# Attention and MLP kernel: weight loads in written order, six staging buffers, VectorE and ScalarE by hand in batch 0, and k, q, p turned on VectorE

## The chip, the cores and the metric

The kernel runs on one core of one Trainium2 chip. The metric is device time in microseconds (us) of one execution. A core has four engines that matter here: TensorE (PE, matrix products; PEld is its weight load), VectorE (DVE), ScalarE (ACT) and GpSimd (POOL), and SyncE (SP), whose queue issues all the DMA transfers of this kernel. Each engine works through its own list of instructions in order and waits at semaphores for the others.

## The reference

Eight batches, eight heads, 576 positions, 64 wide. Each head has 32 rows p, which attend to k and v; q then attends to the 32 packed rows. The heads side by side are the input of an MLP with the function h * tanh(softplus(h)).

```python
def sm_attn(qq, kk, vv):
    s = scale * np.matmul(qq, kk.transpose(0, 1, 3, 2))
    s = s - np.max(s, axis=-1, keepdims=True)
    a = np.exp(s)
    a = a / (np.sum(a, axis=-1, keepdims=True) + 1e-09)
    return np.matmul(a, vv)
p_packed = sm_attn(p, k, v)
out = sm_attn(q, p_packed, p_packed)
...
h = x @ w_in                      # 4608 x 512 @ 512 x 2048
sp = np.where(h > 20.0, h, np.log1p(np.exp(np.minimum(h, 20.0))))
g = h * np.tanh(sp)
return (g @ w_out).astype(np.float32)
```

q, k, v, p are float32; w_in and w_out are float64 and are made float32 on the chip.

## The kernel before, in words

**Weights.** A piece of a weight matrix is 128 x 512 float64, loaded as 128 x 1024 int32 into a staging buffer `w_st` (L343 for w_in, L370 for w_out; three buffers, `STB`). ScalarE takes its two words apart (`words`, L350 and L351), VectorE joins them into a float32 (`join`, four instructions in a chain on the same tile: L355, L358, L359, L362). There are 32 pieces: 16 of w_in (named wi) and 16 of w_out (named wo).

**Attention.** k and q come as tiles of 96 partitions (`load_heads`, L103, 288 KB a transfer). PE transposes them in blocks of four (`transposed`, L129), and ScalarE or VectorE copies each block out of PSUM (L119 to L123). p is transposed by PE too (L177) and copied by VectorE (L180, L183). Then PE makes the scores (L138); VectorE takes the maximum and subtracts it (L192 to L196); ScalarE takes the exponentials (L231) and VectorE their sums (L232); PE transposes the weights (`turn_weights`, L241, twelve per batch) and makes the packed rows (`values`, L250); these are scaled (L258), transposed (L266) and copied (L267) into ppT. The second half multiplies ppT with qT (L138), turns the result with VectorE's own transposes (`match`, L281), normalizes (`peak` and `weigh`, L289 to L302), turns it back (L307), and splits it in a high and a low part, aT_hi on ScalarE (L308) and aT_lo on VectorE (L309).

**MLP.** The packed rows stand before the weights: `packed_w` (L380) multiplies ppT with a quarter of w_in and splits the result into wp_hi (ScalarE, L391) and wp_lo (VectorE, L392). There are four quarters a batch. A group (b, f) is one batch and 128 of the 2048 hidden columns: `up` makes 2 x 6 products of 288 columns (L430), ScalarE applies the function (L433, L435), and from batch 1 on `halves` splits the result into g_hi (L444) and g_lo (L445) on VectorE. `down` multiplies with w_out: in batch 0 in float32 (L469), later as three split products (L449, L450, L451). The split of w_out (wo_hi on ScalarE, L92, and wo_lo on VectorE, L93) stands in batch 1's loop. Every sixteenth group `evac` copies four accumulators into `o` (three buffers) and out. Each batch leaves 64 of its 576 positions over; two batches' rests are multiplied together (L449 to L451 with the names r_hi, r_lo, ps_rest).

**Order.** After batch 0's attention the loop runs over t = 0 .. 129: up of group t, down of group t - 2, and between them up to three steps of the next batch's attention, a generator. PE's order is as written throughout. The other engines are ordered by hand through batch 0's attention, and after it by the tile scheduler, which by its own estimate places each engine's instructions. In batch 0's loop each step converts two pieces.

## Time and profile before

| | |
|---|---|
| median of 3 runs | 825.61 us (821.64 to 1091.88) |
| profiled execution | 823.42 us |
| its span | 821.5 us |
| PE busy | 768.5 us (94%) |
| PE weight load busy | 592.8 us (72%) |
| VectorE busy | 407.3 us (50%) |
| ScalarE busy | 335.0 us (41%) |
| DMA by SP's queue | 55.59 MB, 24.0% of 16 engines' span |

The profile is one execution. The span runs from the first instruction to the last; the execution's time is 1.92 us longer. In a row of the timeline stand the start, the duration, the engine, the line, the operation with its result and operands, the shape, how many follow one another, and in brackets the idle time before it and what ended that. In a row of a group stand the number of instructions, their busy time and mean, and the idle time before them by what ended it. Two PE matmuls overlap, so the distance between their starts is shorter than their durations.

### The profile page before, as it was taken

To read this page: it belongs to the slowest core of one execution; us is meant where nothing else is said; L and a number is where in the kernel's file an instruction comes from. 1 tells how busy PE (TensorE), PEld (TensorE's weight loads), DVE (VectorE), ACT (ScalarE), POOL (GpSimd) and SP (SyncE) were. 2 spreads that over 40 slices of the span, in tenths; PEclk is the share of its full clock that TensorE was granted. 3 is DMA by queue.
4 is the path that set the end of the run, shared out by engine and by line. 5 is a ranking of instruction groups with operands and counts; after the bars stand their busy time and mean duration, and the time that the engine had idled before them with its cause. 6 is when DMAs were issued, how large, how long until landed. Compare 5 with 4: busy or idle time off the path is not lost.

```text
span 821.5 us, 13455 instructions
## 1 busy us (share of the span) xinstructions
PE 768.5 (94%) x5520; PEld 592.8 (72%) x5520; DVE 407.3 (50%) x778; ACT 335.0 (41%) x772; POOL 0.7 (0%) x6
## 2 busy tenths in 40 slices
PE   6527779999999999999999999999999999999997
PEld 4305456557878887877878887877878887888886
DVE  4388787634373344634373444634373444633332
ACT  4156576435342352435342352435342352432221
POOL 0000000000000000000000000000000000000000
PEclk7558999999999999999999999999999999999999
DMA  9826773022300332022300332022300300010002
GB/s 241 214 77 212 235 210 113 1 63 83 86 3 1 102 85 59 1 64 81 88 1 1 102 85 59 1 68 78 88 1 1 100 23 2 1 52 1 1 1 64
DMA packets 34748, 56.43 MB, mean 69 GB/s; under 512 B 7552, under 2 KB 25984, under 8 KB 34688
## 3 DMA queue, kind: packets, MB, share of 16 engines
q1 hardware_dynamic: 34688, 55.59, 24.0%
q8 instruction: 43, 0.70, 0.4%
q14 instruction: 17, 0.14, 0.1%
HBM read 46.14 MB, written 9.44 MB: 68 GB/s over the span
## 4 chain that ended last, share of the span: by engine, by line
PE 86%; DMA 5%; DVE 4%; ACT 3%; issue 1%; SPq 0%; DVEq 0%; ACTq 0%
PE ps_h L430 24%; PE acc L449 14%; PE acc L450 13%; PE acc L451 13%; PE acc L469 5%; DMA w_st<-in_moe_w_in_dram 4%; PE ps_kq L129 4%; PE ps_w L380 4%; PE ps_s L138 3%; PE ps_rest L449 2%; PE ps_rest L450 2%; PE ps_rest L451 2%; PE ps_pp L250 2%; PE ps_a L241 1%; DMA w_st<-in_moe_w_out_dram 1%
## 5 line engine op out<-in xcount | busy, mean ns | idle before, releaser
L433 ACT ACTIVATE g<-ps_h 128x288 f32<-128x288 f32 (+1 forms) x256 | 98.6, 386 | 275.5 <-PE ps_h L430 240.8
L449 PE MATMUL acc<-wo_hi,g_hi 128*128 128x512 f32 x448 | 186.6, 417 | 0.0
L450 PE MATMUL acc<-wo_lo,g_hi 128*128 128x512 f32 x448 | 176.2, 393 | 0.0
L451 PE MATMUL acc<-wo_hi,g_lo 128*128 128x512 f32 x448 | 175.8, 392 | 0.0
L430 PE MATMUL ps_h<-aT_hi,wp_hi 128*128 128x288 f32 x512 | 166.9, 326 | 9.4 <-ACT aT_hi L308 6.3
L444 DVE CAST g_hi<-g 128x512 fp32r<-128x512 f32 x112 | 47.7, 426 | 227.4 <-ACT g L433 227.4
L430 PE MATMUL ps_h<-aT_lo,wp_hi 128*128 128x288 f32 x512 | 152.5, 298 | 0.9 <-DVE aT_lo L309 0.9
L430 PE MATMUL ps_h<-aT_hi,wp_lo 128*128 128x288 f32 x512 | 152.2, 297 | 0.6 <-DVE wp_lo L392 0.6
L430 PEld LDWEIGHTS ps_h<-aT_hi,wp_hi 128*128 128x128 f32 x512 | 97.4, 190 | 30.7 <-issue 10.8
L449 PEld LDWEIGHTS acc<-wo_hi,g_hi 128*128 128x128 f32 x448 | 84.1, 188 | 36.6 <-issue 17.3
L430 PEld LDWEIGHTS ps_h<-aT_lo,wp_hi 128*128 128x128 f32 x512 | 97.6, 191 | 13.6 <-issue 5.0
L451 PEld LDWEIGHTS acc<-wo_hi,g_lo 128*128 128x128 f32 x448 | 84.1, 188 | 19.3
L430 PEld LDWEIGHTS ps_h<-aT_hi,wp_lo 128*128 128x128 f32 x512 | 97.4, 190 | 0.9 <-DVE wp_lo L392 0.9
L450 PEld LDWEIGHTS acc<-wo_lo,g_hi 128*128 128x128 f32 x448 | 84.4, 188 | 7.0
L445 DVE TENSOR_TENSOR g_lo<-g,g_hi 128x512 fp32r<-128x512 f32 x112 | 77.2, 689 | 5.9 <-PE ps_kq L129 0.5
L469 PE MATMUL acc<-wo,g 128*128 128x512 f32 x128 | 64.9, 616 | 0.0
L380 PE MATMUL ps_w<-wi,ppT 64*32 64x512 f32 x512 | 37.7, 615 | 14.9 <-DVE wi L362 14.7
L392 DVE TENSOR_TENSOR wp_lo<-ps_w,wp_hi 128x512 fp32r<-128x512 f32 x64 | 41.2, 681 | 19.1 <-ACT wp_hi L391 19.1
L391 ACT CAST wp_hi<-ps_w 128x512 fp32r<-128x512 f32 x64 | 34.3, 588 | 32.3 <-PE ps_w L380 32.3
L129 PEld LDWEIGHTS ps_kq<-ident,k_t 96*128 96x128 f32 x192 | 20.8, 144 | 18.2 <-issue 6.7
L469 PEld LDWEIGHTS acc<-wo,g 128*128 128x128 f32 x128 | 22.0, 196 | 15.3 <-issue 15.2
L129 PE MATMUL ps_kq<-ident,q_t 96*128 96x96 f32 x192 | 25.6, 264 | 7.6 <-issue 5.2
(93 smaller groups left out, 769.8 us busy)
## 6 DMA issues: line engine op xcount, KB each, us to landing
k_t<-in_k_dram SPq DMA_DIRECT2D x32, 288.0 KB, 3.6
v_t<-in_v_dram SPq DMA_DIRECT2D x32, 288.0 KB, 4.0
q_t<-in_q_dram SPq DMA_DIRECT2D x32, 288.0 KB, 4.3
w_st<-in_moe_w_in_dram SPq DMA_DIRECT2D x16, 512.0 KB, 4.8
w_st<-in_moe_w_out_dram SPq DMA_DIRECT2D x16, 512.0 KB, 4.2
out_dram<-o SPq DMA_DIRECT2D x24, 192.0 KB, 2.2
out_dram<-o SPq DMA_DIRECT2D x16, 128.0 KB, 3.3
out_dram<-o SPq DMA_DIRECT2D x24, 64.0 KB, 2.5
```

The lines of the kernel that those rows point to most:

```text
L129: nc.tensor.transpose(out=ps[:, h, :], in_=of_slot(src, g, h)[:, i, :], identity=ident[:R, :R])
L380: nc.tensor.matmul(out=ps[g][h * NP:(h + 1) * NP, :], lhsT=ppTb[row:row + D, g, h * NP:(h + 1) * NP], rhs=wi[c][g][row:row + D, h // 2, :] ...
L391: nc.scalar.copy(out=hi, in_=ps[g])
L392: nc.vector.tensor_tensor(out=lo, in0=ps[g], in1=hi.bitcast(F32), op=ALU.subtract)
L430: nc.tensor.matmul(out=ps, lhsT=w[:, fs], rhs=a[:, g, cs], start=(n == 0), stop=(n == 5))
L433: nc.scalar.activation(out=self.act[:, hf * HALF:hf * HALF + m], in_=ps[:, :m], func=AF.Mish)
L444: nc.vector.tensor_copy(out=hi, in_=self.act)
L445: nc.vector.tensor_tensor(out=lo, in0=self.act, in1=hi.bitcast(F32), op=ALU.subtract)
L449: nc.tensor.matmul(out=acc, lhsT=hi[:, cs], rhs=wh, start=start, stop=False)
L450: nc.tensor.matmul(out=acc, lhsT=hi[:, cs], rhs=wl, start=False, stop=False)
L451: nc.tensor.matmul(out=acc, lhsT=lo[:, cs], rhs=wh, start=False, stop=stop)
L469: nc.tensor.matmul(out=accs[c], lhsT=grp.act[:, cs], rhs=wo[f], start=f == 0, stop=f == NF - 1)
```

## The change

**Opening.** SP runs by hand, in the order of the program, through the whole of batch 0; VectorE and ScalarE are placed by the scheduler in batch 0's attention, which is written in another order (the first half's second product ahead of the second half's values), and by hand in the loop of batch 0, up to t = 16. There are six staging buffers in place of three. The weights are taken in the order w_in's first quarter, then a piece of w_in and one of w_out by turns; a step joins two, and the words of the piece after are taken behind each join. Batch 0's q, k, v, p lie in a pool `early` of their own, closed at t = 1 (`LOAD0`), when the first three of the later batches' tiles are asked for; the others follow as tiles come free (`load_next`).

**Batches 1 to 7.** A class `Later` loads k and q with 32 columns at a time on 32 partitions (four transfers of 32 x 4 x 544 a tile, in two lanes that overlap, so that they are loaded twice), v on 2 x 64 partitions, p in four transfers. VectorE turns k and q in one STREAM_TRANSPOSE a tile (`lanes`, L374 of the changed kernel, 128 x 1152) and p in one (L368). The weights of the first softmax are turned in ten 128-wide transposes instead of twelve, the packed rows made in 40 matmuls instead of 48 per half. VectorE's work on a PE result is written after the next PE work (`pending`, `flush`).

**Else.** w_out is split from t = 14 on (`SPLIT0`), the first eight into a pool `late`; two output buffers instead of three; rows go out in groups of 64.

```diff
-KVB = 8
-STB = 3
-OB = 3
+KQB = 3
+STB = 6
+OB = 2
+ATT0 = 4
+LOAD0 = 1
+HALFWAY = 8
+SPLIT0 = 14
...
+        def load_side(self, src, g, tag):
+            t = kv[0].tile([P, 4, NX, D], F32, name=tag, tag="kqv", bufs=KQB)
+            for w in range(2):
+                for e in range(2):
+                    lane = (2 * w + e) * NP
+                    rows = src[self.b, 4 * g:4 * g + 4, w * HALF:(w + 1) * HALF].rearrange("h (p x) d -> p h (x d)", x=NX)
+                    nc.sync.dma_start(
+                        out=t[lane:lane + NP].rearrange("p h x d -> p h (x d)")[:, :, :NX * D - NP],
+                        in_=rows[:, :, e * NP:e * NP + NX * D - NP],
+                    )
+            return t
...
+        def lanes(self, src):
+            t = att.tile([P, 4, HALF], F32, name="xT", tag="T", bufs=2)
+            nc.vector.transpose(
+                out=t.rearrange("a h (x n) -> a (h x) n", n=NP),
+                in_=src.rearrange("a h x (e d) -> a (h x) e d", e=2)[:, :, 0, :],
+            )
+            return t
...
-    weights = [Weight(0, m) for m in range(4)] + [WeightOut(0)] + [Weight(1, m) for m in range(4)]
-    weights += [WeightOut(i) for i in range(1, 4)] + [Weight(2, m) for m in range(4)]
-    weights += [WeightOut(i) for i in range(4, 8)] + [Weight(3, m) for m in range(4)]
-    weights += [WeightOut(i) for i in range(8, NF)]
...
+    pieces = [Weight(0, m) for m in range(4)]
+    for f in range(NF):
+        if f < 12:
+            pieces.append(Weight(1 + f // 4, f % 4))
+        pieces.append(WeightOut(f))
...
+    def join_next(n):
+        for _ in range(n):
+            k = pieces_done["join"]
+            upto("words", k + 1)
+            upto("join", k + 1)
+            upto("fetch", k + 1 + STB)
+            upto("words", k + 2)
...
+        by_hand.enter_context(tc.manual_schedule(engines={mybir.EngineType.DVE, mybir.EngineType.Activation}))
+        upto("fetch", 4 + STB)
+        upto("words", 5)
...
-                if f == (0 if b else 2) and b + 1 < B:
+                if f == (1 if b else ATT0) and b + 1 < B:
                     gen = batches[b + 1].attention()
-                if f == 10 and b + 2 < B:
-                    batches[b + 2].load()
+                if t == LOAD0:
+                    opening.close()
+                    kv.append(ctx.enter_context(tc.tile_pool(name="kv", bufs=2, side="left", reuse_waits="tile")))
+                    for _ in range(KQB):
+                        load_next()
...
-            if b == 0:
-                convert(2)
-            elif t == NF:
+            joins = 2 if t < 14 else 0
+            if t == NF:
+                by_hand.close()
+            if t == SPLIT0:
                 stage.close()
-                late.append(ctx.enter_context(tc.tile_pool(name="late", bufs=1)))
-            if b == 1:
-                split_wo(f)
+                late.append(ctx.enter_context(tc.tile_pool(name="late", bufs=1, side="right", reuse_waits="tile")))
+            if 0 <= t - SPLIT0 < NF:
+                split_wo(t - SPLIT0)
```

**What moves on the engines.** On SP, in the opening, before: from the third weight piece (L343 loads w_in, L370 w_out, L103 k, q and v, L165 p).

```order
L343 DMA w_st<-in_moe_w_in_dram 128x1024
L165 DMA p_t<-in_p_dram 128x2x64 x2
L103 DMA q_t<-in_q_dram 96x2x384 x2
L343 DMA w_st<-in_moe_w_in_dram 128x1024
L370 DMA w_st<-in_moe_w_out_dram 128x1024
L103 DMA k_t<-in_k_dram 96x2x384 x4
L103 DMA q_t<-in_q_dram 96x2x384 x2
L343 DMA w_st<-in_moe_w_in_dram 128x1024
L103 DMA q_t<-in_q_dram 96x2x384 x2
L343 DMA w_st<-in_moe_w_in_dram 128x1024 x3
```

The same place now (L521 loads w_in, L548 w_out, L117 batch 0's k, q and v; L355 and L324 the later batches' p, and k and q):

```order
L117 DMA q_t<-in_q_dram 96x2x384 x2
L521 DMA w_st<-in_moe_w_in_dram 128x1024 x3
L548 DMA w_st<-in_moe_w_out_dram 128x1024
L521 DMA w_st<-in_moe_w_in_dram 128x1024
L548 DMA w_st<-in_moe_w_out_dram 128x1024
L521 DMA w_st<-in_moe_w_in_dram 128x1024
L548 DMA w_st<-in_moe_w_out_dram 128x1024
L521 DMA w_st<-in_moe_w_in_dram 128x1024
L548 DMA w_st<-in_moe_w_out_dram 128x1024
L355 DMA p_n<-in_p_dram 32x8x32 x4
L324 DMA k_n<-in_k_dram 32x4x544 x8
L324 DMA q_n<-in_q_dram 32x4x544 x4
```

Batch 1's first k and q, eight transfers, stood ahead of the sixth piece and among those that follow; now its first loads stand behind the twelfth piece, all together.

On VectorE, in the joins of batch 0's loop, before (ISA is the last step of a join, the add, L362; the number in a tile's name tells tiles apart):

```order
L355 TENSOR_SCALAR wo_538<-wo_538 128x512
L362 ISA wo_256<-wo_256,wround 128x1024
L358 TENSOR_SCALAR wo_538<-wo_538 128x512
L359 SCALAR_TENSOR_TENSOR wo_538<-w_st,wo_538 128x512
L355 TENSOR_SCALAR wo_548<-wo_548 128x512
L362 ISA wo_538<-wo_538,wround 128x1024
L358 TENSOR_SCALAR wo_548<-wo_548 128x512
L355 TENSOR_SCALAR wo_576<-wo_576 128x512
```

and now (L533, L536, L537, L540 are the four steps):

```order
L533 TENSOR_SCALAR wo_153<-wo_153 128x512
L536 TENSOR_SCALAR wo_153<-wo_153 128x512
L537 SCALAR_TENSOR_TENSOR wo_153<-w_st,wo_153 128x512
L540 ISA wo_153<-wo_153,wround 128x1024
L533 TENSOR_SCALAR wi_0_93<-wi_0_93 128x512
L536 TENSOR_SCALAR wi_0_93<-wi_0_93 128x512
L537 SCALAR_TENSOR_TENSOR wi_0_93<-w_st,wi_0_93 128x512
L540 ISA wi_0_93<-wi_0_93,wround 128x1024
```

Two joins were interleaved; now each runs through its four steps before the next begins.

On VectorE at the end of batch 0, before: the two wp_lo (L392) of batch 1's first quarter, behind that batch's last attention steps (L302, L307, L309) and two single splits of w_out (L93).

```order
L302 TENSOR_TENSOR a_1258<-a_1258,sm_1327 128x1152
L307 STREAM_TRANSPOSE at<-a_1258 128x576
L93 TENSOR_TENSOR wo_lo<-wo_1216,wo_hi 128x512
L309 TENSOR_TENSOR aT_lo<-at,aT_hi 128x576
L307 STREAM_TRANSPOSE at<-a_1258 128x576
L309 TENSOR_TENSOR aT_lo<-at,aT_hi 128x576
L93 TENSOR_TENSOR wo_lo<-wo_1226,wo_hi 128x512
L392 TENSOR_TENSOR wp_lo<-ps_w_1417,wp_hi 128x512
```

and now (L106 is the split of w_out, L583 of a rest, L570 wp_lo), behind the last join:

```order
L540 ISA wo_1151<-wo_1151,wround 128x1024
L106 TENSOR_TENSOR wo_lo_1317<-wo_153,wo_hi_1316 128x512
L106 TENSOR_TENSOR wo_lo<-wo_807,wo_hi 128x512
L106 TENSOR_TENSOR wo_lo_1390<-wo_476,wo_hi_1389 128x512
L106 TENSOR_TENSOR wo_lo_1420<-wo_514,wo_hi_1419 128x512
L106 TENSOR_TENSOR wo_lo_1485<-wo_575,wo_hi_1484 128x512
L106 TENSOR_TENSOR wo_lo_1562<-wo_619,wo_hi_1561 128x512
L106 TENSOR_TENSOR wo_lo_1618<-wo_678,wo_hi_1617 128x512
L583 TENSOR_TENSOR r_lo<-g_rest_481,r_hi 128x4x64
L106 TENSOR_TENSOR wo_lo_1671<-wo_739,wo_hi_1670 128x512
L106 TENSOR_TENSOR wo_lo<-wo_864,wo_hi 128x512
L570 TENSOR_TENSOR wp_lo<-ps_w_1341,wp_hi 128x512
```

Nine splits of w_out and one of a rest now stand directly ahead of wp_lo, and the last steps of batch 1's attention ahead of the last two joins.

More of the change, by code (lines that the diff above doesn't have):

```diff
@@ L325, in attention, with columns @@
+            self.a2 = att.tile([P, 2, S // NP, NP], F32, name="a2", tag="a", bufs=1)
             for g in range(2):
-                yield from self.values(g, ps_a)
-            for g in range(2):
-                yield from self.turn_values(g, ps_a)
-            for g in range(2):
-                yield from self.match(g, ps_a)
+                self.match(g)
+                yield
+                flush()
+                yield
             self.peak(slice(0, 2))
+            yield
             self.weigh(slice(0, 2))
+        def columns(self, a):
+            return a.rearrange("a (x u n) -> a u x n", u=2, n=NP)
@@ L334, in body, with rows, rest_rows @@
+        def rows(self, c):
+            return [(out_x[self.b, 2 * c + e], e * NQ, (e + 1) * NQ) for e in range(2)]
+        def rest_rows(self):
+            return out_x[self.b, NX - 1]
     class Weight:
@@ L474, in down @@
         o = evac(accs[c], c)
[L475 to L481 removed]
+        for dst, lo, hi in batches[b].rows(c):
+            nc.sync.dma_start(out=dst, in_=o[lo:hi, :])
     rest = {}
@@ L578, in body @@
-        convert(4)
-        batches[1].load()
+        by_hand = ExitStack()
+        by_hand.enter_context(tc.manual_schedule(engines={mybir.EngineType.SP}))
+        first.k_t = [load_heads(k, 0, 0, "k_t")]
+        first.load_p()
+        upto("fetch", 1)
+        first.k_t.append(load_heads(k, 0, 1, "k_t"))
+        first.v_t = [load_heads(v, 0, 0, "v_t")]
+        first.q_t = [load_heads(q, 0, 0, "q_t")]
+        upto("fetch", 2)
+        first.v_t.append(load_heads(v, 0, 1, "v_t"))
+        first.q_t.append(load_heads(q, 0, 1, "q_t"))
@@ new lines, in body @@
+        upto("fetch", STB)
+        first.start(ps_a)
+        score = [first.score_now(g) for g in range(2)]
+        for _ in range(3):
+            next(score[0])
+        upto("words", 1)
+        next(score[0], None)
+        upto("join", 1)
+        next(score[1])
+        next(score[1])
+        together(first.turn_weights(0, ps_acc, ("ACT", "ACT")))
+        next(score[1])
+        next(score[1], None)
+        together(first.values(0, ps_a))
+        together(first.turn(0, ps_acc, ("ACT", "ACT", "ACT")))
@@ new lines, in body @@
+        together(first.turn_values(0, ps_a))
+        together(first.turn_weights(1, ps_acc, ("ACT", "ACT")))
+        together(first.match(0, ps_acc))
+        upto("words", 2)
+        first.peak(slice(0, 1))
+        upto("join", 2)
+        together(first.values(1, ps_a))
+        together(first.turn(1, ps_acc, ("ACT", "ACT", "ACT")))
+        together(first.turn_values(1, ps_a))
+        together(first.match(1, ps_acc))
+        upto("words", 3)
+        first.peak(slice(1, 2))
+        first.weigh(slice(0, 1))
@@ L608, in body @@
                 grp.up(0)
-            next(gen, None)
+            chunk = b == 0 and f % 4 == 3 and f < NF - 1
+            if not chunk:
+                advance(gen)
+            join_next(joins - joins // 2)
             if dn:
```

321 lines of the change are left out of this document (207 added, 114 removed).

## The prediction

> **What bounds the kernel now.** I read the windows first: start:end in us, length, then busy time and (instructions) of PE, of PE's weight loads, VectorE, ScalarE, GpSimd, then the granted clock, the DMA engines' busy share and GB/s.
>
> ```profile
> 0.00:20.00 20.00, 11.92 (x86) 8.69 (x86) 8.59 (x25) 8.33 (x19) 0.70 (x6) 0.80 0.94 240
> 40.00:60.00 20.00, 3.68 (x9) 1.05 (x9) 17.44 (x34) 8.94 (x16) 0.00 (x0) 0.50 0.26 79
> 60.00:80.00 20.00, 14.27 (x71) 9.77 (x71) 17.21 (x37) 13.37 (x28) 0.00 (x0) 0.83 0.67 202
> 80.00:100.00 20.00, 17.33 (x96) 9.60 (x96) 16.74 (x36) 11.90 (x26) 0.00 (x0) 0.91 0.68 221
> 100.00:120.00 20.00, 12.91 (x69) 8.06 (x70) 16.03 (x35) 15.11 (x28) 0.00 (x0) 0.91 0.75 214
> 120.00:140.00 20.00, 20.00 (x180) 12.98 (x181) 17.32 (x35) 16.17 (x38) 0.00 (x0) 1.00 0.52 154
> 640.00:740.00 100.00, 99.98 (x742) 80.75 (x741) 45.15 (x82) 38.42 (x92) 0.00 (x0) 1.00 0.13 37
> ```
>
> There are two programs in one. From 120 us to the end PE is never idle, so a microsecond of PE work removed there is a microsecond of time, as long as nothing new makes PE wait. Before 120 us PE waits, and VectorE is the fullest engine (17.4, 17.2, 16.7, 16.0 of 20). The border between the two I put at the first split matmul of batch 1's second product, which I call T0:
>
> ```profile
> 184.65 0.48 PE L449 MATMUL acc<-wo_hi,g_hi 128*128 128x512 f32 x1
> ```
>
> From T0 to the span's end (821.5) are 636.85 us. The timeline of the opening shows why PE is so late at first:
>
> ```profile
> 38.58 0.66 ACT L350 ACTIVATE wi<-w_st 128x512 f32<-128x512 f32 x1 [9.87 <-DMA w_st<-in_moe_w_in_dram]
> ...
> 39.27 0.43 DVE L355 TENSOR_SCALAR wi<-wi 128x512 f32<-128x512 f32 x1 [9.05 <-ACT wi L350]
> ...
> 57.11 0.78 DVE L307 STREAM_TRANSPOSE at<-a 128x576 f32<-128x576 f32 x1
> ...
> 59.73 0.66 ACT L308 CAST aT_hi<-at 128x576 fp32r<-128x576 f32 x1
> ...
> 60.44 0.61 PE L430 MATMUL ps_h<-aT_hi,wp_hi 128*128 128x288 f32 x1 [6.34 <-ACT aT_hi L308]
> 61.95 0.61 PE L430 MATMUL ps_h<-aT_lo,wp_hi 128*128 128x288 f32 x1 [0.90 <-DVE aT_lo L309]
> 62.35 0.44 PE L430 MATMUL ps_h<-aT_hi,wp_lo 128*128 128x288 f32 x1
> 62.59 0.44 PE L430 MATMUL ps_h<-aT_hi,wp_hi 128*128 128x288 f32 x1
> ...
> 66.80 0.30 PE L430 MATMUL ps_h<-aT_hi,wp_hi 128*128 128x288 f32 x1
> 66.93 0.29 PE L430 MATMUL ps_h<-aT_lo,wp_hi 128*128 128x288 f32 x1
> ```
>
> ScalarE waits 9.87 us for the fourth weight piece, whose load stands on SP behind batch 1's k and q, and VectorE, in order, waits 9.05 us with it. PE flows only from 61.95 us, at first with a matmul each 0.24 us, and 0.13 us from 66.8.
>
> **The opening (gain about 14 us).** SP now has pieces 1 to 8 ahead of every load of batch 1. Up to the fourth piece some 5.8 MB are asked for; at the 240 GB/s of the first window that is 24 us, so the 9.05 us go. The second cast of aT_hi came 1.8 us after its transpose (57.89 to 59.73) behind conversions of weights, the first some 0.8 us: 2.6 us, gone since batch 0's attention has fewer of them in its way. In the VectorE groups from 39.2 to 61.9 us stand four kinds of join instructions:
>
> ```profile
> L359 DVE SCALAR_TENSOR_TENSOR wi<-w_st,wi 128x512 int32<-128x512 int32 x4 | 2.7, 685 | 0.0
> L355 DVE TENSOR_SCALAR wi<-wi 128x512 f32<-128x512 f32 x5 | 2.1, 425 | 11.0 <-ACT wi L350 11.0
> L358 DVE TENSOR_SCALAR wi<-wi 128x512 int32<-128x512 int32 x5 | 2.1, 416 | 0.1
> L362 DVE CUSTOM_DVE_ANT_0 wi<-wi,wround 128x1024 uint16<-128x1024 uint16 x3 | 2.0, 684 | 0.1
> ```
>
> That is 8.9 us; the new order keeps two of them there (1.4 us), so 7.5 go. Against this the second half's values, q turn and match now come after the first half's match: about 6 us later, an estimate from the opening's own pace. First full flow: 61.95 - 9.05 - 2.6 - 7.5 + 6 = 48.8, say 48.5 us.
>
> From there VectorE goes by hand, and that decides the rest of batch 0. A join is four instructions, each on the tile the one before wrote:
>
> ```profile
> 25.71 0.42 DVE L355 TENSOR_SCALAR wi<-wi 128x512 f32<-128x512 f32 x1
> 26.16 0.43 DVE L358 TENSOR_SCALAR wi<-wi 128x512 int32<-128x512 int32 x1
> 26.63 0.69 DVE L359 SCALAR_TENSOR_TENSOR wi<-w_st,wi 128x512 int32<-128x512 int32 x1
> 27.46 0.69 DVE L362 CUSTOM_DVE_ANT_0 wi<-wi,wround 128x1024 uint16<-128x1024 uint16 x1
> 28.07 0.48 DVE L267 COPY ppT<-ps_ppT 128x128 f32<-128x128 f32 x2
> ```
>
> From start to next start 25.71 to 28.07 = 2.36 us. Twenty-seven joins stand after batch 0's attention: 63.7 us. Between them stand batch 1's attention and part of batch 2's:
>
> ```profile
> L307 DVE STREAM_TRANSPOSE at<-a 128x576 f32<-128x576 f32 x16 | 12.4, 775 | 0.3
> L289 DVE TENSOR_REDUCE mx<-a 128x36 f32<-128x1152 f32 x7 | 9.5, 1353 | 0.2
> L392 DVE TENSOR_TENSOR wp_lo<-ps_w,wp_hi 128x512 fp32r<-128x512 f32 x64 | 41.2, 681 | 19.1 <-ACT wp_hi L391 19.1
> L93 DVE TENSOR_TENSOR wo_lo<-wo,wo_hi 128x512 fp32r<-128x512 f32 x16 | 10.4, 684 | 6.1 <-PE acc L469 5.0 <-ACT g_rest L435 1.1
> ```
>
> A lane (a transpose of 128x1152) isn't in the trace: between 1.35 (as L289's 1152 elements) and 1.55 us (twice L307's 576); I take 1.4, since a fixed part is paid once. Six lanes are 8.4, two turns of p (256 elements) 0.9, the five wide operations of 1152 elements 6.8, and the rest of that attention (spread, normalize, copies, blocks, the two halves of aT) 11: 27 us. Three wp_lo pairs are 4.1, with a wait of about 1.5 each, since VectorE now stands there while PE makes the product and ScalarE the cast (the row's 19.1 us over 32 pairs is 0.6, a lower bound): 4.5. And one more wait: on SP 3.5 MB of batch 1's loads stand ahead of the thirteenth piece. Issued near 50 us, they land near 65 at 240 GB/s, the piece at 69, its conversion at 70; VectorE wants it at 67. I take 4 us, and 2 for p of batch 2. Last join: 48.5 + 63.7 + 27 + 4.1 + 4.5 + 6 = 153.8 us.
>
> Then the order of VectorE has nine wo_lo splits and one r_lo before wp_lo of batch 1's first quarter: 10 x 0.6 + 1.4 = 7.4, so 161.2 us. PE, which has its work up to group 16 done near 151, stands there for some 10 us. Behind the wait queue groups 16 and 17 with their fp32 second product, about 7.5 us, and about 2 us are lost on a slow clock: T0 = 170.7, against 184.65 a gain of 14. The bounds are 150 (PE alone) and 185 (loads at half the rate), the first two rivals.
>
> The slow clock after a wait is in the rows above (0.24, then 0.13 us a matmul, after a window at 0.50). The Trainium skill, in "TensorE: Matmul & The Clock Gate", Part 1, says that PE runs at half rate until a window of some 3.4 us has been busy; the trace agrees (62.35 to about 66).
>
> **The steady part (gain about 25 us).** Each batch had 48 PE transposes of k and q, in 12 blocks of four. One block, in the timeline at 271 us:
>
> ```profile
> 271.14 0.39 PE L451 MATMUL acc<-wo_hi,g_lo 128*128 128x512 f32 x1
> 271.38 0.49 PE L129 MATMUL ps_kq<-ident,k_t 96*128 96x96 f32 x4
> 271.65 0.38 PE L430 MATMUL ps_h<-aT_hi,wp_hi 128*128 128x288 f32 x1
> 271.87 0.30 PE L430 MATMUL ps_h<-aT_lo,wp_hi 128*128 128x288 f32 x1
> ```
>
> The L451 would be followed at its own pace of 0.23; the flow is back at 271.87 less the 0.13 of an up matmul: 271.74 - 271.37 = 0.37 us for four. Twelve are 4.4 us a batch. The rest comes from the groups:
>
> ```profile
> L241 PE MATMUL ps_a<-ident,a 128*96 128x128 f32 x96 | 16.7, 291 | 0.5 <-ACT a L218 0.5
> L250 PE MATMUL ps_pp<-v_t,a1T 96*32 96x64 f32 x768 | 15.3, 233 | 0.7 <-DVE a1T L123 0.7
> L177 PE MATMUL ps_p<-ident,p_t 128*128 128x128 f32 x16 | 3.1, 273 | 1.1 <-DMA p_t<-in_p_dram 1.1
> ```
>
> Over 8 batches: two of 12 turns of weights 0.35, 8 of 48 values 0.3, p 0.4; these busy times overlap their neighbours, so I take 0.8 for the three. That is 5.2 us of PE a batch. After T0 run five whole attentions (26 us) and what is left of batch 2's; before, part of that stood ahead of T0, so it gives 2.7. Together 28.7.
>
> What it adds lies on VectorE: four lanes and one turn of p, 6.1 us a batch less 0.5 of copies, on an engine that is busy 45 of 100. Its cover is PE's queue: a group's g_hi and g_lo are wanted two groups later, some 10 us, while a lane holds VectorE for 1.4. The uncovered place is wp_lo, which PE wants soon after it makes the product:
>
> ```profile
> L129 PE MATMUL ps_kq<-ident,k_t 96*128 96x96 f32 x192 | 24.4, 253 | 8.8 <-DVE wp_lo L392 4.1 <-DMA k_t<-in_k_dram 2.7 <-issue 1.9
> ```
>
> Only 4.1 us of waiting on it now, in the whole program. Nothing lost is one bound; the other, every lane of six batches in the way, is 24 x 1.4 = 34. I take 0.6 a batch and 0.5 at the end for two output buffers instead of three: 4. Steady: 636.85 - 28.7 + 4 = 612.2. ScalarE loses twelve copies a batch, which gives nothing.
>
> Sum: span 170.7 + 612.2 = 782.9; the profiled run took 1.92 us more than its span (823.42 against 821.5): **785 us**. That run lies 0.3% under the median of 825.61.
>
> Against the change speaks how k and q are loaded: twice the bytes, in four transfers of 32 partitions. Now a weight piece on 128 partitions takes this long:
>
> ```profile
> w_st<-in_moe_w_in_dram SPq DMA_DIRECT2D x16, 512.0 KB, 4.8
> ```
>
> In the Trainium skill, "SBUF — State Buffer", Door 1, a transfer into 32 partitions reaches 8 of 16 ports and moves 189 GB/s where 128 partitions move 328. By that page the 3.5 MB would take 18.5 us instead of 14.6 and the sum would be 789. No run here shows it yet; the four transfers of a tile go to all four quarters and may overlap, so I keep the row's rate and the rival below.
>
> **The rivals.**
> *A: VectorE keeps up, PE bounds batch 0.* From 60 to 184.65 us PE was busy 14.27 + 17.33 + 12.91 + 64.65 = 109 us; without the transposes and batch 2's part 101. From 48.5 that ends at 150, so 150 + 612.2 + 1.9 = 764. For it: joins of different tiles could run closer, and waits may lie beside one another. Against: 63.7 us of joins are measured in series.
> *B: narrow loads at half rate.* At 120 GB/s the 3.5 MB take 29 us, the thirteenth piece is 14 us later, everything by hand behind it too: T0 185, 799 us. For it: small rows, one queue; against: 202 to 221 GB/s in the windows above with 96-partition loads among the pieces.
> *C: VectorE becomes the wait in the steady part.* If the lanes cost PE 30 of the possible 34 us, 785 + 26 = 811, about no change. For it: in its order a lane of q stands ahead of a spread; against: half of VectorE is free.
> *D, the other side: the pieces are fetched one by one.* By hand, a piece that is late stops wp_lo, spread and the halves of aT behind it. If the loads of batch 1 hold the slots so that each of the 27 joins pays its piece's 4.8 us, not 2.36, that is 66 us more: T0 237, 851 us. It decides once a piece costs over 3.9 us (T0 past 212). For it: one queue in written order; against: six slots keep five pieces in flight.
>
> **How the numbers follow.** Chances: forecast 0.58, A 0.16, B 0.14, C 0.08, D 0.04. The forecast's own bounds are the 6 us of load waits (0 to 14) and the steady waits (0 to some 12); with A and B inside, the range is 760 to 812. Two per cent, about what can be told from no change, is 809 to 842: the forecast, A and B lie below (0.88), C and a mild D within (0.09), D above (0.03).
>
> **What would show it.** Right: PE's first up matmul in full flow near 48 us; no PE transposes of k, q and p in batches 1 to 7; joins in fours at 2.36 us; T0 at 165 to 178 with a PE wait of some 10 us on wp_lo before it; 605 to 620 us from there to the end. Wrong: T0 near 150 (A), or over 185 with VectorE waiting for ScalarE's conversions and those for w_st (B, D), or PE idle on wp_lo or g_lo after 200 us (C).

## The result, and the profile after

The changed kernel takes 789.91 us (median of 4 runs, 787.66 to 792.87), the kernel before in the same comparison 825.29 us. One of its four runs was slow, at 1091.88 us, and the ratio leaves it out: 0.959, with an interval of 0.954 to 0.964, some 34 us, 4%. The profiled execution took 790.09 us, with a span of 788.3 us.

| us, of the profiled execution | before | predicted | after |
|---|---|---|---|
| PE's first full flow | 61.95 | 48.5 | 45.96 |
| from there to T0 | 122.7 | 122.2 | 126.4 |
| T0 | 184.65 | 170.7 | 172.34 |
| from T0 to the span's end | 636.85 | 612.2 | 616.0 |
| execution | 823.42 | 785 | 790.09 |

The windows of the kernel after, with the columns of the prediction's first fence (the last two are the DMA engines' share and GB/s):

```profile
40.00:60.00 20.00, 16.10 (x66) 10.62 (x66) 16.22 (x31) 13.36 (x28) 0.00 (x0) 0.75 0.47 111
60.00:80.00 20.00, 13.91 (x71) 7.24 (x70) 14.19 (x26) 7.13 (x16) 0.00 (x0) 0.91 1.05 292
...
120.00:140.00 20.00, 20.00 (x115) 10.77 (x114) 17.30 (x31) 11.52 (x24) 0.00 (x0) 1.00 1.06 236
140.00:160.00 20.00, 14.63 (x56) 7.39 (x54) 16.75 (x25) 13.20 (x26) 0.00 (x0) 0.83 0.16 37
...
640.00:740.00 100.00, 100.00 (x690) 81.34 (x689) 42.59 (x73) 31.55 (x83) 0.00 (x0) 1.00 0.05 11
```

PE works in the window of 40 to 60 us, where it stood before (16.1 of 20, was 3.7). A hole stays at 60 to 80 us (13.9, was 14.3), and a new one has come at 140 to 160 us (14.6), where PE was full before; lower granted clocks stand beside them (0.91 and 0.83). The DMA engines, busy for 0.5 to 0.75 of the time from 60 to 140 us before, are now full there. In the last row PE has 690 matmuls in 100 us, where it had 742: the transposes, which are short, are gone, and what is left is longer on average.

PE's timeline in the opening, with every wait of over 2 us from the first flow to T0:

```profile
45.96 0.61 PE L608 MATMUL ps_h<-aT_lo,wp_hi 128*128 128x288 f32 x1 [0.18 <-DVE aT_lo L296]
...
62.13 1.05 PE L558 MATMUL ps_w<-wi,ppT 64*32 64x512 f32 x6 [2.07 <-DVE wi L540]
...
79.92 1.35 PE L385 MATMUL ps_s<-xT,pT 64*32 64x288 f32 x16 [4.01 <-DVE a L405]
...
82.08 0.44 PE L608 MATMUL ps_h<-aT_hi,wp_hi 128*128 128x288 f32 x1
82.32 0.44 PE L608 MATMUL ps_h<-aT_lo,wp_hi 128*128 128x288 f32 x1
...
98.20 1.93 PE L558 MATMUL ps_w<-wi,ppT 64*32 64x512 f32 x6 [4.35 <-DVE wi L540]
...
145.14 0.40 PE L608 MATMUL ps_h<-aT_hi,wp_hi 128*128 128x288 f32 x1 [2.79 <-ACT g L611]
...
152.14 0.45 PE L608 MATMUL ps_h<-aT_hi,wp_hi 128*128 128x288 f32 x1 [2.58 <-ACT g_rest L613]
...
172.34 0.79 PE L627 MATMUL acc<-wo_hi,g_hi 128*128 128x512 f32 x1
```

Five waits of 2.1 to 4.4 us each, and after those that end at 79.92 and 98.20 the next `up` matmuls follow each other at 0.24 us again, not 0.13. From 45.96 to 172.34 us PE was busy 109.7 us and idle 16.7. Before, in the stretch from 61.95 to 184.65, it was 108.6 and 14.1. So the opening's gain of 12.3 us is a flow that starts 16.0 us earlier, less 3.7 us that the stretch behind it has grown.

Where ScalarE and VectorE stand in that stretch, from their timelines:

```profile
47.86 0.43 DVE L533 TENSOR_SCALAR wo<-wo 128x512 f32<-128x512 f32 x1 [1.95 <-ACT wo L528]
50.22 0.42 DVE L533 TENSOR_SCALAR wi<-wi 128x512 f32<-128x512 f32 x1
...
71.52 0.69 ACT L528 ACTIVATE wi<-w_st 128x512 f32<-128x512 f32 x1 [6.48 <-DMA w_st<-in_moe_w_in_dram]
72.24 0.43 DVE L533 TENSOR_SCALAR wi<-wi 128x512 f32<-128x512 f32 x1 [3.25 <-ACT wi L528]
...
104.35 0.45 DVE L368 STREAM_TRANSPOSE pT<-p_n 128x256 f32<-128x256 f32 x1 [6.21 <-DMA p_n<-in_p_dram]
...
142.20 1.16 ACT L278 ACTIVATE a<-a 128x1152 f32<-128x1152 f32 x1 [3.68 <-DVE a L275]
143.38 1.28 ACT L611 ACT_TABLE_LOAD   x1
```

From one join to the next are 50.22 - 47.86 = 2.36 us. The thirteenth piece holds ScalarE for 6.48 us and VectorE for 3.25; the spread of scores behind it on VectorE is what PE waits for at 79.92. The turn of batch 2's p holds VectorE for 6.21 us: PE has work just then and loses 0.18 us at once, but all of VectorE's list behind it is that much later. At 142 us ScalarE, by hand, waits 3.68 us for the end of the subtraction, takes the exponentials and loads a table, and only then, from 144.68 us, applies the function g that PE waits for (the 2.79 us at 145.14).

### The profile page after: what moved, and what is told of

Read it like the earlier page. It is cut to its first block, busy times and chain, and to the rows that moved or that the text cites. A ratio compares the mean times of both kernels' runs of the same rounds, so it can differ in the third digit from the quotient of the medians.

```text
span 788.3 us, 12461 instructions
## 1 busy us (share of the span) xinstructions
PE 746.2 (95%) x5044; PEld 566.7 (72%) x5044; DVE 442.4 (56%) x788; ACT 298.8 (38%) x685; POOL 0.7 (0%) x6
## 4 chain that ended last, share of the span: by engine, by line
PE 80%; DVE 6%; DMA 6%; ACT 5%; issue 1%; SPq 1%; DVEq 0%; ACTq 0%
PE ps_h L608 24%; PE acc L627 14%; PE acc L628 12%; PE acc L629 12%; PE ps_w L558 4%; DMA w_st<-in_moe_w_out_dram 2%; PE ps_s L385 2%; PE acc L647 2%; PE ps_rest L629 2%; PE ps_rest L628 2%; PE ps_rest L627 2%; DMA w_st<-in_moe_w_in_dram 2%; PE ps_pp L440 1%; DMA q_t<-in_q_dram 1%; DMA p_n<-in_p_dram 1%
## 5 line engine op out<-in xcount | busy, mean ns | idle before, releaser
L627 PE MATMUL acc<-wo_hi,g_hi 128*128 128x512 f32 x448 | 183.8, 410 | 0.0
L647 PE MATMUL acc<-wo,g 128*128 128x512 f32 x128 | 66.8, 642 | 0.0
L570 DVE TENSOR_TENSOR wp_lo<-ps_w,wp_hi 128x512 fp32r<-128x512 f32 x64 | 41.1, 685 | 20.5 <-ACT wp_hi L569 20.5
L558 PE MATMUL ps_w<-wi,ppT 64*32 64x512 f32 x512 | 40.9, 622 | 6.4 <-DVE wi L540 6.4
L647 PEld LDWEIGHTS acc<-wo,g 128*128 128x128 f32 x128 | 24.2, 208 | 17.2 <-issue 15.2
L613 ACT ACTIVATE g_rest<-ps_h 128x64 f32<-128x64 f32 x128 | 28.0, 219 | 0.0
L582 ACT CAST r_hi<-g_rest 128x256 fp32r<-128x256 f32 x32 | 13.1, 408 | 33.6 <-PE ps_rest L628 33.0
## 6 DMA issues: line engine op xcount, KB each, us to landing
w_st<-in_moe_w_in_dram SPq DMA_DIRECT2D x16, 512.0 KB, 10.4
```

The costliest lines, as they stand in the source:

```text
L558: nc.tensor.matmul(out=ps[g][h * NP:(h + 1) * NP, :], lhsT=ppTb[row:row + D, g, h * NP:(h + 1) * NP], rhs=wi[c][g][row:row + D, h // 2, :] ...
L570: nc.vector.tensor_tensor(out=lo, in0=ps[g], in1=hi.bitcast(F32), op=ALU.subtract)
L613: nc.scalar.activation(out=self.g_rest[self.b % 2][self.f // 4][:, self.f % 4, :], in_=ps[:, m:], func=AF.Mish)
L627: nc.tensor.matmul(out=acc, lhsT=hi[:, cs], rhs=wh, start=start, stop=False)
L647: nc.tensor.matmul(out=accs[c], lhsT=grp.act[:, cs], rhs=wo[f], start=f == 0, stop=f == NF - 1)
```

## The experiments

Each is an edit of the changed kernel. Their times are compared with runs of the kernel before beside them, and the ratio is to that. In the traces of kernels that share the opening's order the full flow begins anywhere from 42.6 to 46 us without any edit to it, so for the opening I compare the stretch from full flow to T0 (126.4 us after), and behind it the time from T0 to the end (616.0). That last time is 615.9 to 616.5 us in e2, e3, e5, e6 and e8 as well, which do not touch it: it is a sharper ruler than the total.

**Are PE's transposes the gain in the steady part?** Three kernels put twelve blocks of four PE transposes (of a constant, their result not used) back into each later batch. e1 puts one at each of the first twelve steps of the attention:

```diff
+        def block(self):
+            ps = psum(ps_a, [P, 4, R], "ps_x")
+            for h in range(4):
+                nc.tensor.transpose(out=ps[:, h, :], in_=ident[:R, :], identity=ident[:R, :R])
+
         def attention(self):
+            for n, _ in enumerate(self.steps()):
+                if n < 12:
+                    self.block()
+                yield
```

> The changed kernel, with twelve blocks of four PE transposes (of the identity, into PSUM, read by nobody) put back into the attention of each of batches 1 to 7; the result is the same. Theory: in the steady part PE is the bound and a block costs it 0.35 us, so six batches' blocks give back 6 x 12 x 0.35 = 25 us, and batch 1's fall into waits: about 813 us. Rival: the steady gain came from the copies and waits that went with the transposes, PE had room: under 5 us, below 795.

Measured: 876.07 us, ratio 1.065 [1.062, 1.067], far above what any theory gave. PE's waits from T0 on say why:

```profile
PE ps_x L466 <- DVE a L405: 34.7, 12, 3.3
```

The change writes VectorE's spread of the scores (`a`, L405) behind the next PE work. Until it runs, the scores hold the two buffers of the PSUM pool that my blocks also take. So the experiment built a wait of its own and says nothing of the transposes. The part behind T0 is 81 us longer than in the changed kernel, more than these 34.7 us and the theory's 25 us of blocks; the mean granted clock there is 0.96, and was 1.00. e7 places a block only where no such spread is pending:

```diff
         def attention(self):
+            blocks = 12
+            for _ in self.steps():
+                if blocks and not pending:
+                    self.block()
+                    blocks -= 1
+                yield
+            while blocks:
+                self.block()
+                blocks -= 1
```

> The changed kernel, with the same twelve blocks of four PE transposes a batch as in e1, but only at steps at which no scores wait in PSUM for VectorE. Theory (PE is the bound after batch 0, a block costs it 0.28 to 0.35 us): six batches x 12 blocks = 20 to 25 us, 810 to 815 us, and no wait of PE longer than 1 us after 200 us. Rival (the blocks of e1 cost by themselves, not by the scores' buffers): over 840 us.

Measured: 851.57 us, ratio 1.035 [1.033, 1.037], still far off, and in the range of the rival. But PE's waits from T0 on show a reason like that of e1, and not a price of the blocks:

```profile
PE ps_x L466 <- DVE a L405: 16.1, 12, 2.2
PE ps_x L466 <- DVE wp_lo L586: 12.0, 6, 2.1
```

e9 puts three blocks at once behind each of four lanes, at steps where the pool is free:

```diff
         def attention(self):
+            for n, _ in enumerate(self.steps()):
+                if n in (0, 1, 7, 8):
+                    for _ in range(3):
+                        self.block()
+                yield
```

> The changed kernel, with the twelve blocks of four PE transposes a batch put three each behind the four lanes, where both PSUM buffers have long been read. Theory (PE-bound, 0.28 to 0.35 us a block, and what e1 and e7 showed beyond it was waiting for the scores' buffers): 810 to 815 us, PE's waits as in the changed kernel. Rival (PE has room): under 800 us.

Measured: 819.99 us (8 runs), ratio 0.994 [0.992, 0.996]. This time PE's only wait after T0 is one of 0.8 us, so the price can be read. The blocks behind T0 in the tile view:

```profile
L466 PE MATMUL ps_x<-ident x264: 244/246/248, 196.1 to 668.4; 96*128 96x96 f32 x132
```

264 matmuls are 66 blocks. From T0 to the end are 639.4 us, 23.4 more than after: 0.355 us a block (predicted 0.37). That brings the steady part back to what it was before (636.85), with VectorE's lanes still in place. The total lies 5 us above the expectation, since batch 1's blocks stand in the opening too: 18 of the 84 lie before T0, 6.4 us at that price, and the stretch to T0 grew by 9.5 to 135.9 (PE is busy 5.8 us more there, and idle 3.7 more). Together the blocks cost 31.6 us of span in the two profiled runs, 30 by the medians. **Without the removal of PE's transposes almost nothing of the gain is left: 0.6% of 4%.**

**Is it the order by hand, and the buffers?** e2 leaves VectorE and ScalarE to the scheduler in batch 0's loop:

```diff
-        by_hand.enter_context(tc.manual_schedule(engines={mybir.EngineType.DVE, mybir.EngineType.Activation}))
```

> The changed kernel, with VectorE and ScalarE ordered by the tile scheduler in batch 0's loop too (SP by hand, six buffers and all else as they are). Its order puts some 40 join instructions ahead of the last half of aT: theory (VectorE's list decides batch 0): the first group's flow comes 15 to 20 us later than 46 us, and the split product of batch 1 5 to 12 us later: 795 to 803 us. Rival (bytes decide, the order on VectorE does not matter): 787 to 792 us.

Measured: 815.65 us, ratio 0.993 [0.990, 0.995]: the direction was right, the size is 26 us instead of 5 to 13. One of its windows, and two of PE's waits in the timeline:

```profile
40.00:60.00 20.00, 0.00 (x0) 0.00 (x0) 15.60 (x29) 4.83 (x9) 0.00 (x0) 1.00 1.05 286
```

```profile
62.27 0.61 PE L608 MATMUL ps_h<-aT_hi,wp_hi 128*128 128x288 f32 x1 [24.12 <-ACT aT_hi L295]
...
79.18 0.61 PE L608 MATMUL ps_h<-aT_hi,wp_hi 128*128 128x288 f32 x1 [15.20 <-ACT aT_hi L295]
```

The scheduler puts conversions of weights that have not landed ahead of the casts of aT_hi that PE waits for, for 24 and 15 us. Full flow starts at 79.97 us, T0 is 198.2, and behind it the kernel is the same (615.9 us). e3 keeps three staging buffers, so the fetches of the fifth and sixth pieces move behind the first joins:

```diff
-STB = 6
+STB = 3
...
         upto("join", 1)
+        upto("fetch", 4)
...
         upto("join", 2)
+        upto("fetch", 5)
```

> The changed kernel with three staging buffers instead of six. Theory: with three, a piece's next load is asked for only two joins ahead, and with some 10 us from issue to landing a piece costs 4 to 5 us instead of 2.4: 805 to 818 us. Rival (the DMA engines are full from 60 to 140 us anyway, so more requests ahead bring nothing): 788 to 794 us.

Measured: 809.21 us, ratio 0.984 [0.982, 0.986], inside the expectation. ScalarE waits 33.1 us for w_out's pieces there, and that comes back as waits of PE:

```profile
PE ps_w L558 <- DVE wi L540: 24.5, 3, 16.8
```

So T0's 172 us needs the written order and the six buffers together: without the one it is 198, without the other 190, and the kernel before had 185. Neither e2 nor e9 is the kernel before with half of the change: by the total e2 keeps 0.7% and e9 0.6% of the 4%, and such shares don't add up. The profile's split does: 12.3 us up to T0 and 20.85 behind it.

**Where does the stretch up to T0 lose its time?** e4 keeps VectorE and ScalarE by hand for two more steps, so that the scheduler does not bring batch 2's turn of p forward among the joins:

```diff
-            if t == NF:
+            if t == NF + LAG:
                 by_hand.close()
```

> The changed kernel, with VectorE and ScalarE by hand two steps longer, to t = 18, so that batch 2's p and k turns no longer stand among batch 0's joins. Theory (VectorE's list, in order, sets the end of batch 0): the 6.2 us of waiting for p and the 3.2 us of turns go out of the list, the last join comes some 9 us sooner and batch 1's first split product 4 to 8 us sooner: 782 to 786 us. Rival (DMA bandwidth sets it, 1.0 of the engines busy from 60 to 140 us): the same bytes must come, the wait moves to a conversion: 788 to 791 us.

Measured: 790.13 us, ratio 0.960 [0.958, 0.962]: no gain, and in the rival's range. T0 came 6.0 us earlier (166.37), as the theory said; but 2.2 of these lie before full flow, so the stretch is 3.8 us shorter. From T0 on it took 620.8 us, 4.8 more, and three quarters of that is one row of PE's timeline:

```profile
175.06 0.59 PE L627 MATMUL acc<-wo_hi,g_hi 128*128 128x512 f32 x1 [3.62 <-DVE o L636]
```

VectorE's copy of `o` waits there for a transfer out of the buffer (3.06 us), and with it PE. There are two output buffers, as in the changed kernel, where this copy waits 0.41 us. What differs is SP's queue. Batch 2's p and k are turned later here, so the loads that follow them are asked for later, and stand among the output's transfers:

```profile
165.32 1.96 SPq L324 DMA_DIRECT2D q_n<-in_q_dram  x4
167.38 2.29 SPq L654 DMA_DIRECT2D out_dram<-o  x4
```

The eight output transfers of batch 0 land 6.0 us after their issue in the median. In the changed kernel, where no load stands among them, they take 2.4 us. e10 takes e4 with three output buffers, for which two small tiles had to go:

```diff
-OB = 2
+OB = 3
...
-    still = const.tile([P, P], F32, name="still")
-    nc.vector.memset(still, 0.0)
...
-            mx = stat.tile([P, 2 * (S // NP)], F32, name="mx2")[:, :G]
+            mx = stat.tile([P, 2 * (S // NP)], F32, name="mx2", bufs=1)[:, :G]
...
-            sm = stat.tile([P, 2 * (S // NP)], F32, name="sm2")[:, :G]
+            sm = stat.tile([P, 2 * (S // NP)], F32, name="sm2", bufs=1)[:, :G]
...
-            nc.tensor.matmul(out=ps_warm, lhsT=still, rhs=still, start=True, stop=True)
+            nc.tensor.matmul(out=ps_warm, lhsT=ident, rhs=ident, start=True, stop=True)
...
-            if t == NF:
+            if t == NF + LAG:
```

> e4 (by hand to t = 18) with three output buffers; the room comes from the tile of zeros for the first matmuls and two small tiles. Theory (e4 won 5.9 us up to batch 1's first split product and lost it to one wait of 3.1 us for an output buffer and what stood behind it): 784 to 787 us. Rival (the loads that e4 moved behind batch 0 cost elsewhere): 788 to 791 us.

Measured: 797.86 us, ratio 0.972 [0.967, 0.976], a miss: the wait for `o` is gone, and another has taken its place, in VectorE's timeline:

```profile
189.97 0.45 DVE L366 STREAM_TRANSPOSE pT<-p_n 128x256 f32<-128x256 f32 x1 [8.43 <-DMA p_n<-in_p_dram]
```

Now it is batch 3's p, whose load stands on SP behind transfers that wait themselves. VectorE stands at it with the splits of g behind it, and PE waits 4.5 us for g_hi. From T0 on this kernel takes 624.7 us. e8 leaves e4 aside and spreads the first three loads of batch 1 over three steps, so that the thirteenth piece comes earlier:

```diff
-                    for _ in range(KQB):
-                        load_next()
+                if LOAD0 <= t < LOAD0 + KQB:
+                    load_next()
```

> The changed kernel, with batch 1's first three tiles asked for at t = 1, 2 and 3, one each, instead of all at t = 1, so that one and not three stand ahead of the thirteenth weight piece. Theory (that piece's lateness, ScalarE's 6.5 and VectorE's 3.2 us of waiting near 70 us, is 4 us of the end of batch 0): 784 to 788 us. Rival (what is won there is lost at the later tiles or at batch 2's p, since the bytes are the same): 789 to 793 us.

Measured: 795.99 us, ratio 0.968 [0.964, 0.972]. ScalarE's wait for the piece went (it is converted at 61.2 us, without one), but the rival's price came, and more of it than the rival said; two of the waits between 40 and 180 us:

```profile
DVE pT L368 <- DMA p_n<-in_p_dram: 13.0, 1, 13.0
...
PE ps_h L608 <- DVE wp_lo L570: 8.4, 1, 8.4
```

The bytes have to come in any case. Moved off the piece, they are late for batch 2's p, and VectorE, in order, passes that on to wp_lo. The two edits together are e11, which is e10 with the loads spread:

```diff
-                    for _ in range(KQB):
-                        load_next()
+                if LOAD0 <= t < LOAD0 + KQB:
+                    load_next()
```

> e10 with batch 1's first three tiles asked for one a step (e8). Theory (e8 won the lateness of the thirteenth piece and lost it to batch 2's p, which VectorE no longer meets in this list): 2 to 6 us under e10, 779 to 785 us. Rival (the bytes decide: what comes sooner for the one piece comes later for others): as e10 or slower.

Measured: 798.32 us, ratio 0.970 [0.967, 0.972]; the same waits as e10 (8.2 us on p_n, 4.3 on g_hi), T0 172.33, nothing won. e5 asks whether the joins' 63.7 us in series hold T0 up. It runs two joins interleaved, both at one place of the step, with the fetches behind both:

```diff
+        upto("words", k + 2)
+        for steps in zip(*(x.join_steps() for x in pieces[k:k + 2])):
+            for step in steps:
+                step()
+        pieces_done["join"] = k + 2
+        upto("fetch", k + 2 + STB)
+        upto("words", k + 3)
...
-            join_next(joins - joins // 2)
+            join_next(joins)
...
-            join_next(joins // 2)
```

> The changed kernel, with the two joins of a step interleaved, so that no instruction needs the one just before it: about 1.9 us a join instead of 2.36. Theory (VectorE's list): 27 x 0.45 = 12 us less on it, batch 1's first split product up to 10 us sooner, 780 to 784 us. Rival (bytes): VectorE waits for the conversions instead, 787 to 791 us.

Measured: 798.4 us, ratio 0.970 [0.968, 0.972], slower than both theories said. The joins did run closer. VectorE, ScalarE and PE in its timeline:

```profile
51.89 0.42 DVE L537 TENSOR_SCALAR wi<-wi 128x512 f32<-128x512 f32 x1
...
55.64 0.42 DVE L537 TENSOR_SCALAR wi<-wi 128x512 f32<-128x512 f32 x1
...
70.10 0.66 ACT L528 ACTIVATE wi<-w_st 128x512 f32<-128x512 f32 x1 [13.23 <-DMA w_st<-in_moe_w_in_dram]
...
71.84 0.61 PE L612 MATMUL ps_h<-aT_hi,wp_hi 128*128 128x288 f32 x1 [8.77 <-ACT wp_hi L573]
```

A pair takes 55.64 - 51.89 = 3.75 us, 1.88 a join instead of 2.36. But the thirteenth piece, again behind 16 transfers on SP, lands at 70 us, ScalarE now waits 13.2 us for it, and the cast of wp_hi that stands behind it in ScalarE's list holds PE for 8.8 us. A shorter chain on VectorE only came sooner to the same transfer, with worse work behind it. (The edit also moves both joins of a step to one place; what that alone costs was not tried.)

e6 takes the bytes themselves away: the second lanes of batches 1 and 2 are zeroed by GpSimd, not loaded.

```diff
+                    if e and self.b < 3:
+                        nc.gpsimd.memset(t[lane:lane + NP].rearrange("p h x d -> p (h x d)"), 0.0)
+                        continue
```

> The changed kernel, with the second lanes of k and q of batches 1 and 2 (half of the eight tiles' bytes, 4.5 MB) set to zero by GpSimd instead of loaded; those two batches' attention is then not the reference's. Theory (VectorE's list): only its waits for data go, 6.2 and 3.2 us: 781 to 786 us. Rival (bytes): 4.5 MB at the 265 GB/s of 60 to 140 us are 17 us: 773 to 778 us.

Measured: 795.19 us, ratio 0.966 [0.964, 0.968]. It settles nothing on the bytes, since GpSimd disturbs VectorE, told under the hardware below; its stretch up to T0 begins 1.8 us late (47.76) and is 3.9 us longer.

e12 goes to the two waits at 145 and 152 us. It is e4 with two buffers for p, and the end of an attention (maximum and subtraction, exponentials, sums and multiplication, turn, casts into aT_hi and aT_lo), two pieces of work before, written as steps, so that ScalarE's function for a group stands between the exponentials and the casts of aT_hi:

```diff
-            self.peak(slice(0, 2))
+            yield from self.finish_weights()
+
+        def finish_weights(self):
...
+            yield
+            nc.scalar.activation(out=a2, in_=a2, func=AF.Exp, scale=scale)
             yield
-            self.weigh(slice(0, 2))
...
+            for g in range(2):
+                at = att.tile([P, S], F32, name="at", bufs=1)
+                nc.vector.transpose(out=at, in_=self.a2[:, g].rearrange("a g n -> a (g n)"))
+                yield
...
-            self.p_t = kv[0].tile([P, H, NP], F32, name="p_n", bufs=1)
+            self.p_t = kv[0].tile([P, H, NP], F32, name="p_n", bufs=2)
```

> e4 (by hand to t = 18) with two tiles for p in place of one, and the end of the later batches' attention in steps of its own: VectorE's maximum and difference, then ScalarE's exponential one step on, the sums and the first turn another step on, each half of aT one more. So the function of a group no longer stands behind an exponential that waits for VectorE. Theory (in the changed kernel PE's two waits of 2.8 and 2.6 us near 142 and 150 us are ScalarE standing at the exponential and at the two casts): neither wait over 1.5 us, batch 1's first split product near 162 us, 780 to 786 us. Rival (VectorE's list decides, and what ScalarE gains it waits for elsewhere): 787 to 792 us.

Measured: 786.93 us (784.13 to 788.53), ratio 0.955 [0.953, 0.958]. T0 is 163.2, full flow 45.05: the stretch is 118.2 us, 8.2 less than after. The longer of the two waits that were at 145 and 152 us, and the one that is long now, in PE's timeline:

```profile
150.24 0.40 PE L633 MATMUL ps_h<-aT_hi,wp_hi 128*128 128x288 f32 x1 [0.58 <-ACT g_rest L638]
...
172.73 0.80 PE L652 MATMUL acc<-wo_hi,g_hi 128*128 128x512 f32 x1 [4.44 <-DVE o L661]
```

The two waits are down to 0.4 and 0.6 us, and T0 is near the 162 of the theory; what the second tile for p gives alone was not run. The wait for wp_lo, which the prediction had put at 10 us, shows here with 1.1. Then the output buffers take 4.4 us of it back, and from T0 on are 622.0 us, so the time lies between the theory's range and the rival's. It is the fastest version measured, some 3 us under the changed kernel, but the two intervals overlap; that it is faster is likely, and not shown.

## Why the prediction was right, and where it was not

**The time.** 785 was predicted, 790 came. The two gains of the forecast happened, and none of the four rivals; one step between them, PE's wait for wp_lo, did not. The miss of 5 us has two parts: T0 1.6 us late, and 3.8 us in the steady part.

**The start of the flow: right in kind, 2.5 us too cautious.** Pieces 1 to 8 ahead of batch 1's loads take away the 9.05 us wait: ScalarE converts the fourth piece at 25.54 us and without a wait, where it was 38.58 after 9.87. The casts of aT_hi come within 0.1 us of their transposes, and two join instructions are left in VectorE's list there, both as predicted. 48.5 was predicted for full flow; 45.96 came here, and 42.6 to 46 in the experiments that share this opening. With these three terms as taken the flow would start at 42.8 us (61.95 - 9.05 - 2.6 - 7.5), so the later match cost about 3 us, and the 6 set against the gain for it were the term that was too large.

**The joins, the thirteenth piece: right; the wait for p: too small.** 2.36 us a join, as predicted. ScalarE converts the piece at 71.5 (predicted 70), since SP issues it behind 16 transfers. SP's queue in the timeline of after:

```profile
49.92 1.90 SPq L355 DMA_DIRECT2D p_n<-in_p_dram  x4
51.87 3.79 SPq L324 DMA_DIRECT2D k_n<-in_k_dram  x8
56.23 3.86 SPq L324 DMA_DIRECT2D q_n<-in_q_dram  x4
61.13 0.35 SPq L521 DMA_DIRECT2D w_st<-in_moe_w_in_dram  x1
```

VectorE waited 3.25 us there (4 were taken). For batch 2's p 2 us were taken, and 6.2 came: it stands on the same queue behind pieces and v. The last join ends at 155.9, not 153.8. The lanes were sized well:

```profile
L374 DVE STREAM_TRANSPOSE xT<-k_n x14: 1334/1336/1372, 67.7 to 577.5; 128x1152 f32<-128x1152 f32 x14
```

1.34 us for a tile of k (and 1.37 for one of q), against bounds of 1.35 and 1.55 and 1.4 taken.

**The step that failed: PE standing for 10 us at wp_lo.** VectorE was done with wp_lo of batch 1's first quarter at 163.1 us (161.79 + 1.28), nearly when predicted (161.2):

```profile
155.91 4.42 DVE L106 TENSOR_TENSOR wo_lo<-wo,wo_hi 128x512 fp32r<-128x512 f32 x7
...
161.79 1.28 DVE L570 TENSOR_TENSOR wp_lo<-ps_w,wp_hi 128x512 fp32r<-128x512 f32 x2
```

But PE was not there waiting. It began the group that needs wp_lo at 162.15 us and came to wp_lo itself at 162.82, with no idle time before it:

```profile
162.15 0.70 PE L608 MATMUL ps_h<-aT_hi,wp_hi 128*128 128x288 f32 x1
...
162.82 0.29 PE L608 MATMUL ps_h<-aT_hi,wp_lo 128*128 128x288 f32 x1
```

The prediction had PE ready "near 151", which it doesn't work out; for rival A it took 101 us of PE work from full flow to T0. PE was busy 109.7 us, and lost 15.8 us in the five waits of the timeline, nearly all of its 16.7 us of idle time. T0 came out nearly right for another reason: the sum goes by VectorE's list, which ends 1.9 us from where it was put, and from there to T0 it took 9.3 us, against 9.5. That PE's own list, some 11 us later than predicted, comes to wp_lo at the same moment is luck: later still, it would have moved T0. The busy time is larger than taken in part since the waits are followed by matmuls at 0.24 us: the mean granted clock over the stretch is 0.90, where it was 0.95 before. An estimate from the two clocks (0.10 of 126.4 us less 0.05 of 122.7) is 6.5 of the 8.7 us; the rest is open. The prediction looked at VectorE's list for the waits, and not at ScalarE's: of the five, three end with an instruction of VectorE, and the two at 145 and 152 us come from what stands ahead of the group's function on ScalarE, and e12, which puts the function ahead, makes the stretch 8.2 us shorter, of which e4's edit, part of it, gives 3.8.

**The steady part: right in kind, two terms mis-sized with opposite signs.** The start of one packed_w of a pair of batches, to the same place two batches later, first before, then after:

```profile
262.80 1.09 PE L380 MATMUL ps_w<-wi,ppT 64*32 64x512 f32 x16
...
447.43 1.09 PE L380 MATMUL ps_w<-wi,ppT 64*32 64x512 f32 x16
```

```profile
249.30 1.09 PE L558 MATMUL ps_w<-wi,ppT 64*32 64x512 f32 x16
...
425.50 1.09 PE L558 MATMUL ps_w<-wi,ppT 64*32 64x512 f32 x16
```

184.6 and 176.2 us, so 4.2 a batch. Twelve blocks at e9's 0.355 are 4.3, as much as the whole gain. The 0.8 us taken for the turns of the weights, the values and p together don't show; for the values at least there was nothing to win, since in these two stretches PE is busy 3.6 us with the 160 matmuls of now, and was 3.5 with the 192 of before. Five whole attentions give 21 instead of 26 us, and the 2.7 for what is left of batch 2's did not show (T0 need not cut that attention at the same step in the two programs: before had 69 blocks behind it, e9 has 66). At 0.355 us the 69 blocks are 24.5 us, 3.6 more than the 20.85 that came; PE's idle time behind T0 has grown from 4.5 to 6.6 us, and the rest is open. Against that, the 4 us taken for new waits did not come either: from T0 on the list of PE's waits is empty in the trace of after. 28.7 - 4 was predicted, 20.85 came. Rival C is out with that: VectorE is busy 42.6 of 100 us in the late window, lanes and all.

**Rival B, narrow loads at half rate, is refuted.** Between 54 and 61 us only transfers of k and q of 32 partitions are under way: SP issued them from 51.9 to 60.1 us with nothing else between. Of what was issued ahead of them, the piece landed 3.6 us after its issue at 49.54 us, and p's last transfer by about 54.8 us (it is 32 KB); the next piece was issued only at 61.13. The windows there:

```profile
54.00:58.00 4.00, 4.00 (x19) 2.59 (x18) 3.62 (x8) 2.46 (x7) 0.00 (x0) 1.00 1.04 242
58.00:62.00 4.00, 2.05 (x13) 0.35 (x11) 3.62 (x7) 0.98 (x2) 0.00 (x0) 1.00 1.06 232
```

They move 242 and 232 GB/s, as much as the first window before (240), and the rival wanted 120. The Trainium skill, in "SBUF — State Buffer", Door 1, gives 189 GB/s for a transfer into 32 partitions, and under "Can I just issue two DMAs to hit both halves?" says that two transfers side by side gain only 6% over one. The measurement decides: four transfers to the four quarters of a tile, many in flight, moved over 230. The rate of one alone was not tried. The loads put more bytes on the one queue (77.6 MB instead of 55.6), and with them there a piece of w_in lands after 10.4 us in the median, where it took 4.8:

```profile
w_st<-in_moe_w_in_dram SPq DMA_DIRECT2D x16, 512.0 KB, 10.4
```

**Rivals A and D.** A needed PE without waits; its T0 of 150 was not reached by any kernel, 163.2 being the best. For D the pieces would have had to come one by one; one piece was late by 6.5 us, and with three buffers (e3) T0 moved by 18 us, to 190, not past 212.

**What stays open.** How much the doubled bytes cost in the opening: e6 was to say and was disturbed. And whether the gain of e4 and e12 before T0 can be kept behind it: the wait for one of the two output buffers takes 3.6 to 4.4 us back, and the one trial with three (e10) lost 8.4 us of VectorE's time to a late p.

## What to carry to other kernels

Work taken from a full engine is worth its distance between neighbours in the stream (0.355 us for four small matmuls here), and to check it by putting the work back, the added work must not take a buffer that something deferred still holds. When an engine's list is written by hand, every transfer that it waits for, on any of the engines in the chain, becomes a wait of all that stands behind it: write down arrival against need for each before believing a shorter chain, as e5, e8 and e10 each moved a wait and gained nothing. And a time that comes out right is no proof of its steps: here a 10-us wait at one place was five waits of 2 to 4 us at others, and two engines' lists happened to end together.
